# Pooled attention and grouped experts: K's sums turned by VectorE after a trip through DRAM, six weight buffers, halved subtractions, new orders

## The chip, the cores and the metric

The kernel runs on one core of one Trainium2 chip. The metric is the device time of one execution in microseconds (us); lower is better. Runs are compared with runs of the kernel before on the same chip.

## The reference, cut to what matters

Attention over pooled keys and values, then a layer of 16 experts in 4 groups, of which each token uses one:

```python
# q, k, v: (8 batches, 8 heads, 576, 64), float32
k_p = k.reshape(B, H, 72, 8, D).mean(axis=3)          # K and V pooled by 8
v_p = v.reshape(B, H, 72, 8, D).mean(axis=3)
scores = matmul(q, k_p.T) / 8
attn = exp(scores - max); attn /= attn.sum() + 1e-9
x = matmul(attn, v_p)  -> (4608 tokens, 512)
g = argmax(x @ w_group); e = argmax(x @ w_expert[g])   # the token's group and expert
out = softmax weight of g * softmax weight of e * (relu(x @ w1[g, e]) @ w2[g, e])
# w1[g, e]: 512 x 1024, w2[g, e]: 1024 x 512
```

## The kernel before

**Batches and pieces.** The work of a batch (576 tokens) is cut into pieces, methods of `Att` (attention and routing) and `Moe` (the experts). `main_expert` (L459) finds the expert that most tokens of the batch chose; `Moe` computes the whole batch with it. What other experts are owed is done at the end by `Left` in blocks of 32 rows. Three batches are in flight: in the strings that set the order, `a` and `m` are attention and experts of batch b, `n` and `w` those of b+1, `x` the attention of b+2, `t` the opening's odd jobs and `l` the leftover.

**Order.** Nothing is scheduled by the compiler. Four strings, `START`, `FIRST` (batch 0), `STEADY` (batches 1 to 6) and `LAST` (batch 7), name the pieces one by one, and each engine and each DMA queue takes its instructions in that order. An instruction that waits holds up everything behind it on its engine. Nearly all loads are issued by SP (SyncE), stores of the output by ScalarE's queue.

**K.** `load_k` fetches K; `kr` (L225, by `total`, L211) and `rr` (L230) sum 8 neighbours into `kp` and `rp`. For the scores, K must have the head dimension on the partitions: `kt` (L263) does that on TensorE, for batch 0 by matmuls against the identity, for the others by two transposes (L268) and two small matmuls (L264); `kta` (L277) brings the result to SBUF on ScalarE and scales it by 1/64 (L288, L292 for batches 1 to 7). `q` of batches 1 to 7 is loaded in pieces of 32 columns (`load_qb`, 4 DMAs of 72 KB a piece, L209) and turned by VectorE (`qb`, L309).

**The rest of the attention.** `sc` (L320) scores on TensorE; `mx`, `sb`, `su_` (L326, L333, L342 to L344) maximum, subtraction and sum on VectorE; `ex` (L337) the exponential on ScalarE; `nm` (L349) the division on POOL (GpSimd); `pt` (L355) a turn on VectorE. `vr` sums V and `rep` (L244, L247), `repa` (L253), `repd` (L261) spread it. `av` (L374) multiplies by V on TensorE; `ava` (L388) and `avd` (L392) split the result into two fp32r parts, `xr` (L399) adds them again on POOL into buffers of the pool `sw`, `rt` (L408) computes the routing's logits on TensorE, `route` (L425 to L449), `count` (L455, L457), `main_expert`, `elect` (L469 to L474) and `gates` (L510 to L521) are small VectorE steps. `elect` ends with a register that SP reads, from which the weight loads take the address.

**The experts.** A weight tile of 512 KB is loaded by `load` (L548, SP) into `sw` (4 buffers), `split` (L555, ScalarE) rounds it to fp32r into `wh`, `spd` (L560, VectorE or POOL) subtracts that into the rest `wl`. There are four tiles of w1 (`1:0` to `1:3`) and four of w2. `up` (L573) multiplies with three products a pair, in 8 rows `f` of two halves (256 and 320 tokens), into a PSUM pool `mm` of 3; `ua` (L578, ScalarE) and `upd` (L583, VectorE) evict it; rows 0 and 1 need tile `1:0`, 2 and 3 `1:1`, 4 and 5 `1:2`, 6 and 7 `1:3`. `down` (L612, L617) has 14 pieces of 8 matmuls, evicted by `da` (L625 to L631) through `y` (3 buffers) and stored. `half` (L586) is a `down` of one chunk for half the columns, used in the last batch. `warm` (L905) runs matmuls on ones.

```python
STEADY = """
m.up:0:0 m.split:1:3 m.ua:0:0 m.up:0:1 n.sc:1 n.qb:2 n.sc:2 n.qb:4 ...
... n.avd:0:0 x.kt x.rep n.avd:0:4 x.qb:0 x.kta n.xr:0 n.xr:2 ... n.rt x.sc:0 ... n.route ...
n.main_expert ... w.load:1:0 n.gex w.load:1:1 m.down:5 w.split:1:0 ... w.spd:1:0:v ... n.gates w.load:1:2 w.spd:1:1:p n.keep_x
"""
```

Of the kernel before, what the change touches and what calls it, by code (L numbers as in the profile page):

```python
# [49 lines left out]
m.load:2:1 m.up:7:1 m.load:2:0 m.split:2:3 n.vr:0 m.up:1:0 m.up:0:0 n.ex:2 n.sc:1 m.upd:6:0 a.rt n.qb:4 m.load:2:2 n.su_:2 n.rep n.sb:0 m.ua:7:1  # L50
m.upd:7:1 x.load_qb:3 n.mx:1 n.nm:2:p m.ua:0:0 n.pt:2 m.spd:2:3:p m.ua:1:0 m.upd:0:0 n.sb:1 m.up:6:1 n.qb:3 m.upd:1:0 n.repa:0 a.route n.ex:0
m.split:2:2 x.load_k:0 x.load_qb:0 m.up:3:1 x.load_k:1 m.ua:6:1 m.ua:3:1 n.ex:1 x.load_v:1 m.split:2:0 n.su_:0 a.count m.up:1:1 n.repa:1 m.up:2:1
m.upd:6:1 n.sc:3 n.repd:1 m.split:2:1 n.sc:4 m.ua:2:1 n.su_:1 m.up:0:1 a.keep_x m.ua:1:1 n.repd:0 n.nm:0:p m.upd:3:1 n.nm:1:p m.upd:2:1 m.spd:2:1:p
m.up:5:1 m.up:4:1 n.mx:4 n.pt:0 m.upd:1:1 n.mx:3 m.spd:2:0:p n.pt:1 m.down:0 n.sb:3 n.sb:4 m.ua:5:1 n.ex:3 m.ua:0:1 n.ex:4 m.ua:4:1 m.upd:5:1
m.upd:0:1 n.su_:4 m.spd:2:2:p n.nm:4:p m.upd:4:1 a.gex n.su_:3 n.nm:3:p m.down:12 x.kr:1:p n.pt:4 m.down:13 n.pt:3 n.av:0:4 x.load_qb:2 x.load_qb:1
n.ava:0:1 x.kr:0:r x.load_v:0 m.down:1 x.rr:r a.gates n.ava:0:4 n.ava:0:0 n.ava:0:3 n.ava:0:2 n.avd:0:4 n.avd:0:0 x.vr:1:p n.avd:0:3 m.da:4 n.avd:0:2
m.down:2 n.xr:0 m.down:9 n.xr:3 x.kt x.qb:0 n.ava:0:5 n.avd:0:1 n.avd:0:5 x.kta n.xr:2 m.down:6 x.vr:0:r x.sc:0 n.xr:1 n.rt x.rep x.mx:0 x.sb:0
# [5 lines left out]
m.up:0:0 m.split:1:3 m.ua:0:0 m.up:0:1 n.sc:1 n.qb:2 n.sc:2 n.qb:4 m.up:1:0 m.ua:0:1 x.load_k:1 m.upd:0:1 x.load_v:0 m.ua:1:0 m.up:2:0 x.load_k:0
m.up:1:1 m.ua:2:0 m.split:1:2 n.qb:3 n.mx:1 m.upd:1:0 m.spd:1:3 m.up:7:0 m.up:3:0 m.up:7:1 n.sc:3 m.upd:2:0 n.sb:1 m.ua:1:1 m.load:2:2 m.spd:1:2
m.upd:0:0 n.mx:2 n.sc:4 m.upd:1:1 n.ex:1 n.sb:2 m.ua:7:0 n.ex:2 n.su_:2 m.split:2:1 m.upd:7:0 n.su_:1 m.ua:3:0 m.up:4:0 m.upd:3:0 m.ua:7:1 m.up:4:1
n.mx:3 m.up:3:1 x.load_qb:0 n.nm:1:p m.load:2:3 m.ua:4:1 m.up:6:0 m.split:2:0 m.ua:3:1 m.upd:7:1 x.load_r:v n.nm:2:p m.spd:2:1:p n.pt:1 m.up:5:0
m.up:5:1 m.up:6:1 m.ua:6:0 n.mx:4 n.sb:3 m.up:2:1 m.upd:4:1 n.pt:2 m.ua:4:0 n.ex:3 m.upd:3:1 m.upd:6:0 n.sb:4 n.su_:3 m.spd:2:0 m.upd:4:0 n.ex:4
n.nm:3:p m.ua:5:0 n.su_:4 m.upd:5:0 m.split:2:2 n.pt:3 m.split:2:3 m.ua:2:1 x.load_r:k n.nm:4:p x.kr:1:p n.pt:4 m.ua:6:1 m.ua:5:1 n.av:0:4 n.ava:0:4
x.vr:0:p m.upd:2:1 m.spd:2:2 n.ava:0:3 m.upd:5:1 x.load_v:1 n.ava:0:0 x.vr:1:p x.rr:r x.load_qb:2 m.upd:6:1 x.load_qb:1 n.ava:0:5 m.down:6 m.down:0
n.avd:0:3 m.spd:2:3:v n.ava:0:2 m.down:7 n.ava:0:1 n.avd:0:1 n.avd:0:2 m.down:8 m.down:12 n.xr:3 n.avd:0:5 x.load_qb:3 m.da:2 m.down:1 n.xr:1 x.kr:0:r  # L70
# [7 lines left out]
l.step m.ua:5:0 l.step m.ua:1:1 m.upd:4:0 l.step m.ua:5:1 m.load:2:3 m.spd:1:3 m.up:6:0 m.upd:5:0 l.step m.split:2:0 m.up:4:1 m.spd:2:0:p l.step
m.ua:0:1 m.up:7:0 l.step l.step m.up:6:1 m.ua:6:0 l.tiles l.which m.split:2:3 m.upd:5:1 m.upd:1:1 m.split:2:2 m.split:2:1 m.upd:0:1 l.fetch_x m.up:7:1
l.fetch_b:1 m.ua:7:0 m.ua:6:1 m.ua:4:1 m.upd:6:0 m.spd:2:1:p m.spd:2:3:p m.ua:7:1 l.slots m.upd:7:0 m.upd:4:1 m.spd:2:2:v l.rows m.upd:6:1 m.down:3  # L80
l.whole:1 l.whole:3 m.down:4 m.down:5 m.upd:7:1 l.whole:0 m.da:1 l.whole:2 l.whole:4 l.turn:0 l.fetch_a:1 l.turn:1 l.turn:3 m.half:3:1 l.turn:2
# [874 lines left out]
```

## Time and profile before

| what | us |
|---|---|
| runs shown: median (lowest to highest of 3) | 559.41 (558.39 to 564.97) |
| the profiled execution | 561.18 |
| its span on the core | 559.1 |
| TensorE busy | 528.1 (94%) |
| VectorE, POOL, ScalarE busy | 364.8, 269.1, 211.7 |

The span goes from the first to the last instruction of the program; 2.1 us lie around it. Busy times are unions of the instructions' spans. A granted clock of 1.00 is full speed. A release behind an idle time ("<-") is inferred from semaphores. In the trace's times, 0 is the span's start.

### The profile page before, as it was taken

To read this page: it belongs to the slowest core of one execution; us is meant where nothing else is said; L and a number is where in the kernel's file an instruction comes from. 1 tells how busy PE (TensorE), PEld (TensorE's weight loads), DVE (VectorE), ACT (ScalarE), POOL (GpSimd) and SP (SyncE) were. 2 spreads that over 40 slices of the span, in tenths; PEclk is the share of its full clock that TensorE was granted. 3 is DMA by queue.
4 is the path that set the end of the run, shared out by engine and by line. 5 is a ranking of instruction groups with operands and counts; after the bars stand their busy time and mean duration, and the time that the engine had idled before them with its cause. 6 is when DMAs were issued, how large, how long until landed. Compare 5 with 4: busy or idle time off the path is not lost.

```text
span 559.1 us, 15184 instructions
## 1 busy us (share of the span) xinstructions
PE 528.1 (94%) x6218; PEld 471.0 (84%) x6218; DVE 364.8 (65%) x940; ACT 211.7 (38%) x402; POOL 269.1 (48%) x212
## 2 busy tenths in 40 slices
PE   3789999999999999999999999999997999979995
PEld 2689887799789998899789988899887987879874
DVE  4789898767656786587467786577667763237620
ACT  2254514454235441544235532545143441334202
POOL 3436395037904684247804593457704652344300
PEclk9679999999999999999999999999998999989999
DMA  9778551680528632781638441894354101724901
GB/s 233 157 192 211 134 111 50 237 284 9 123 64 287 174 71 69 236 240 32 118 109 310 107 93 49 275 335 113 70 184 148 39 2 39 255 94 158 340 12 54
DMA packets 115648, 81.32 MB, mean 145 GB/s; under 512 B 73562, under 2 KB 92250, under 8 KB 115192
## 3 DMA queue, kind: packets, MB, share of 16 engines
q1 hardware_dynamic: 110256, 70.92, 45.6%
...
## 4 chain that ended last, share of the span: by engine, by line
PE 86%; DVE 5%; DMA 4%; ACT 1%; issue 1%; POOL 1%; SPq 0%; ACTq 0%; POOLq 0%; DVEq 0%
PE mm L573 36%; PE mm L612 28%; PE mm L617 5%; PE sc L320 4%; PE sc L374 4%; DMA sw<-in_moe_w_dram 2%; PE tp L408 1%; DMA rem<-in_k_dram 1%; DMA ht<-in_moe_w_expert_dram 1%; PE mm L592 1%; PE sc L244 1%; PE mm L905 1%; PE tp L374 1%; ACT w L555 1%; DVE loh L518 0%
## 5 line engine op out<-in xcount | busy, mean ns | idle before, releaser
L573 PE MATMUL mm<-xt,w 128*128 128x320 f32 (+1 forms) x1536 | 214.6, 300 | 4.1 <-DVE ht L583 4.0
L573 PEld LDWEIGHTS mm<-xt,w 128*128 128x128 f32 x1536 | 208.3, 192 | 6.9 <-DVE ht L583 4.2
L612 PE MATMUL mm<-w,ht 128*128 128x512 f32 x744 | 176.7, 393 | 0.0
L612 PEld LDWEIGHTS mm<-w,ht 128*128 128x128 f32 x744 | 138.1, 188 | 30.9 <-issue 2.1
L560 POOL TENSOR_TENSOR w<-sw,w 128x1024 fp32r<-128x1024 f32 x47 | 113.0, 2413 | 95.8 <-ACT w L555 93.4
L349 POOL TENSOR_TENSOR p<-p,su 128x576 f32<-128x576 f32 (+1 forms) x40 | 45.8, 1150 | 135.4 <-DVE su L344 128.1
L578 ACT ACTIVATE ht<-mm 128x320 fp32r<-128x320 f32 (+1 forms) x128 | 49.5, 408 | 112.6 <-PE mm L573 112.4
L583 DVE SCALAR_TENSOR_TENSOR ht<-mm,ht 128x256 fp32r<-128x256 f32 (+1 forms) x192 | 59.7, 342 | 47.5 <-ACT ht L578 46.1
L555 ACT CAST w<-sw 128x1024 fp32r<-128x1024 f32 x64 | 65.9, 1043 | 27.4 <-DMA sw<-in_moe_w_dram 21.9
L625 ACT ACTIVATE y<-mm,gm 128x512 f32<-128x512 f32 x31 | 21.3, 687 | 69.8 <-PE mm L612 69.8
L399 POOL TENSOR_TENSOR sw<-xt 128x640 f32<-128x640 f32 (+1 forms) x28 | 39.9, 1455 | 7.3 <-DVE xt L392 7.3
L342 DVE TENSOR_REDUCE su<-p 128x8 f32<-128x576 f32 (+1 forms) x40 | 29.8, 744 | 15.2 <-ACT p L337 15.0
L309 DVE STREAM_TRANSPOSE qT<-q 128x512 f32<-128x512 f32 x35 | 24.4, 700 | 20.0 <-PE sc L320 15.1
L218 POOL TENSOR_TENSOR kv<-kv 128x512 f32<-128x512 f32 x21 | 31.9, 1517 | 10.3 <-DMA kv<-in_v_dram 7.9
L560 DVE TENSOR_TENSOR w<-sw,w 128x1024 fp32r<-128x1024 f32 x17 | 28.1, 1654 | 10.9 <-ACT w L555 10.9
L326 DVE TENSOR_REDUCE mx<-sc 128x8 f32<-128x576 f32 (+1 forms) x40 | 29.4, 735 | 6.1 <-PE sc L320 6.1
L355 DVE STREAM_TRANSPOSE pT<-p 128x576 f32<-128x576 f32 (+1 forms) x40 | 30.8, 769 | 3.1 <-POOL p L349 3.1
L617 PE MATMUL mm<-w,ht 128*128 128x512 f32 x128 | 32.4, 397 | 0.0
L337 ACT ACTIVATE p<-p 128x576 f32<-128x576 f32 (+1 forms) x40 | 27.3, 684 | 13.4 <-DVE p L333 9.8
L320 PE MATMUL sc<-kT,qT 64*64 64x72 f32 x1264 | 27.8, 235 | 4.5 <-DVE qT L309 2.9
L374 PE MATMUL sc<-pT,v 32*64 32x128 f32 (+11 forms) x1560 | 30.8, 290 | 1.2 <-DVE m L493 1.1
L320 PEld LDWEIGHTS sc<-kT,qT 64*64 64x64 f32 x1264 | 23.7, 139 | 9.6 <-DVE qT L309 3.1
...
## 6 DMA issues: line engine op xcount, KB each, us to landing
...
```

The lines of the kernel that those rows point to most:

```text
L218: add(out=a[..., 0:256], in0=a[..., 0:256], in1=a[..., 256:512], op=ALU.add)
L320: nc.tensor.matmul(ps[t:t + 64, y, SP * g:SP * g + SP], lhsT=s.qT[c][r, g, w:w + 64], rhs=k, start=True, stop=True)
L349: (nc.vector if eng == "v" else nc.gpsimd).tensor_tensor(out=pf, in0=pf, in1=bc(sf, SP), op=ALU.mult)
L374: nc.tensor.matmul(to[64 * x:64 * x + 64], lhsT=w, rhs=s.pT[e, k, 32 * c0:32 * c0 + n], start=(z == 0), stop=(z == 2))
L399: nc.gpsimd.tensor_tensor(out=x, in0=a, in1=b, op=ALU.add)
L555: nc.scalar.copy(out=wh, in_=raw)
L560: (nc.vector if eng == "v" else nc.gpsimd).tensor_tensor(out=wl, in0=raw, in1=wh.bitcast(F32), op=ALU.subtract)
L573: nc.tensor.matmul(ps[:, 0:n], lhsT=l[:, kc, fs], rhs=xt[:, r, kc, sl], start=(kc == 0 and i == 0), stop=(kc == 3 and i == 2))
L578: nc.scalar.activation(out=s.ht[f][:, o:o + n], in_=s.pu[f, hf][:, 0:n], func=AF.Relu)
L583: stt(out=ht[:, at:at + hi - lo], in0=ps[:, lo - o:hi - o], scalar=0.0, in1=ht[:, lo:hi].bitcast(F32), op0=ALU.max, op1=ALU.subtract)
L612: nc.tensor.matmul(ps, lhsT=s.ht[f][:, 640 * l + o:640 * l + o + 128], rhs=s.w[2, f // 2][r][:, f % 2, :], start=(i == 0), stop=(i == 23))
L617: nc.tensor.matmul(ps, lhsT=s.ht[f][:, 512:640], rhs=s.w[2, f // 2][r][:, f % 2, :], start=(i == 0), stop=(i == 15))
```

## The change

- From batch 1 on, `kt` and `kta` are no longer used. `kw` writes the sums of K to a DRAM buffer `kscr`, `kl` reads them back with 32 positions on the partitions, and `kb` turns them on VectorE in blocks of 32 x 32. `kw` and `kl` are issued by SP.
- 1/64 is no longer multiplied into K by `kta` but given to the exponential as its scale (`ex`), in batch 0 too.
- The pool `sw` has 6 buffers, not 4; `y` has 2, not 3.
- `spd` on POOL is two instructions, each half of the tile (for w1 the halves are the pairs of k chunks that `up` takes in order, for w2 the two rows `f`).
- `FIRST`, `STEADY` and `LAST` are new; `START` isn't changed. `t.warm:8` is no longer in `FIRST`.

```diff
 FIRST = """
-m.split:1:3 a.mx:2 m.up:2:0 n.load_qb:2 m.split:1:2 m.ua:2:0 a.sc:4 a.sb:2 t.warm:8 m.spd:1:2:p m.up:3:0 a.pt:3 m.up:4:0 m.up:5:0 a.ex:2 a.mx:4 a.sb:4
-a.ex:4 m.ua:5:0 n.load_qb:0 a.su_:2 a.nm:2:p a.su_:4 m.ua:3:0 a.nm:4:p m.upd:2:0 a.pt:2 m.split:1:0 a.pt:4 n.rr:r m.ua:4:0 x.load_r:k a.av:2:4
...
+n.load_qb:2 a.sc:4 m.split:1:2 m.split:1:3 a.mx:2 a.sb:2 a.pt:3 a.ex:2 a.mx:4 a.sb:4 m.spd:1:2:p m.split:1:0 m.spd:1:3:v a.su_:2 a.ex:4 n.rr:r
+m.up:3:0 a.su_:4 n.kw a.nm:2:p m.up:5:0 m.ua:3:0 m.ua:5:0 a.nm:4:p n.load_qb:0 m.upd:5:0 m.up:7:0 n.kl a.pt:2 x.load_k:1 m.ua:7:0 m.upd:7:0 m.up:2:0
+m.spd:1:0:p a.pt:4 m.ua:2:0 a.av:2:4 m.up:0:0 m.upd:2:0 a.ava:2:0 n.qb:2 a.ava:2:2 m.upd:3:0 a.ava:2:1 m.load:2:2 x.load_v:1 a.ava:2:3 m.up:1:0
+m.ua:1:0 n.load_v:0 a.avd:2:0 m.ua:0:0 x.load_r:v a.avd:2:2 x.kr:1:p m.load:2:0 a.avd:2:1 n.kb n.qb:1 a.avd:2:3 n.sc:2 m.upd:0:0 x.load_r:k n.sc:1
...
 STEADY = """
...
+m.up:1:0 x.load_qb:2 m.up:0:0 n.sc:1 m.split:1:2 m.ua:0:0 n.qb:2 n.sc:2 m.spd:1:2 m.up:3:0 m.up:4:0 m.ua:1:0 m.up:0:1 m.upd:0:0 m.upd:1:0 m.ua:3:0
...
+n.av:0:4 m.upd:6:1 x.rr:r n.ava:0:1 m.down:6 n.ava:0:4 m.upd:5:1 n.avd:0:1 m.down:12 m.upd:4:1 n.ava:0:5 x.vr:1:p x.load_k:1 m.spd:2:3:v m.down:7
+n.avd:0:4 n.ava:0:2 n.avd:0:5 n.ava:0:0 x.kr:1:p n.ava:0:3 m.down:3 n.xr:1 m.down:8 x.kr:0:r x.load_qb:1 m.da:2 m.down:4 x.load_qb:3 n.avd:0:3 x.rep
+x.repa:1 n.xr:3 n.avd:0:0 n.avd:0:2 n.xr:2 n.xr:0 n.rt n.route m.down:13 m.down:0 x.kw m.da:4 x.kl x.kb n.gex x.repd:1 n.main_expert w.load:1:0
+m.down:1 m.down:9 x.qb:1 x.qb:0 w.load:1:1 x.sc:0 x.mx:0 w.load:1:2 x.sb:0 x.repd:0 w.load:1:3 x.repa:0 x.ex:0 m.down:5 m.down:2 w.load:2:0
+w.split:1:0 m.da:1 m.down:10 m.down:11 n.gates x.su_:0 n.keep_x w.spd:1:0:v w.load:2:1 m.da:0 w.split:1:1 m.da:3 x.nm:0:p x.pt:0 w.spd:1:1:p
 LAST = """
-m.split:1:2 m.up:1:0 m.up:0:0 m.ua:1:0 m.up:3:0 m.up:2:0 m.ua:0:0 m.up:2:1 m.up:3:1 m.ua:3:0 l.xtiles m.split:1:3 l.step l.step m.spd:1:2:p m.up:4:0
...
+m.up:3:0 m.up:2:0 m.up:3:1 m.ua:3:0 m.split:1:3 m.ua:2:0 m.up:1:0 m.up:1:1 m.split:1:2 m.upd:2:0 l.xtiles m.ua:3:1 l.step m.ua:1:0 l.step m.spd:1:2:p
...
+m.down:8 l.fetch_b m.da:4 m.da:2 m.half:3:0
...
+    kscr = dram.tile([B, H * SP, D], F32, name="kscr")
-    sw = ctx.enter_context(tc.tile_pool(name="sw", bufs=4))
+    sw = ctx.enter_context(tc.tile_pool(name="sw", bufs=6))
...
+        def kw(s):
+            to = kscr[s.b].rearrange("(g r) d -> r g d", g=NG)
+            for u in range(2):
+                nc.sync.dma_start(out=to[0:128, u::2], in_=s.kp[:, 2 * u:2 * u + 2])
+            nc.sync.dma_start(out=to[128:144].rearrange("r g d -> g r d"), in_=s.rp[64:128])
+        def kl(s):
+            s.kn = wk.tile([128, 9, 32], F32, name="kn")
+            for y in range(2):
+                for e in range(2):
+                    r = 64 * y + 32 * e
+                    nc.sync.dma_start(out=s.kn[r:r + 32], in_=kscr[s.b, 288 * y:288 * y + 288].rearrange("(k t) d -> t k d", t=32)[:, :, 32 * e:32 * e + 32])
+        def kb(s):
+            s.kT = wk.tile([128, 4 * SP], F32, name="kT")
+            nc.vector.transpose(out=s.kT, in_=s.kn.rearrange("p k d -> p (k d)"))
...
-            nc.scalar.activation(out=p[0:n], in_=p[0:n], func=AF.Exp)
+            nc.scalar.activation(out=p[0:n], in_=p[0:n], func=AF.Exp, scale=1.0 / 64)
...
+            if eng == "v":
+                tt(out=wl, in0=raw, in1=wh.bitcast(F32), op=ALU.subtract)
+                return
+            z = raw.shape[1] // 2
+            for p in (slice(0, z), slice(z, 2 * z)):
+                nc.gpsimd.tensor_tensor(out=wl[:, p], in0=raw[:, p], in1=wh[:, p].bitcast(F32), op=ALU.subtract)
...
-            y = sm.tile([128, DM], F32, name="y", bufs=3)
+            y = sm.tile([128, DM], F32, name="y")
```

## Rows read from the trace of the kernel before

**Rows 1.** The page: busy times of the engines, and the granted clock in 40 slices.
```profile
PE 528.1 (94%) x6218; PEld 471.0 (84%) x6218; DVE 364.8 (65%) x940; ACT 211.7 (38%) x402; POOL 269.1 (48%) x212
...
PEclk9679999999999999999999999999998999989999
```

**Rows 2.** Windows: stretch, us, busy per engine (instructions), granted clock, DMA share, GB/s.
```profile
168.00:196.00 28.00, 28.00 (x308) 26.60 (x308) 19.73 (x52) 14.21 (x24) 15.34 (x8) 1.00 0.75 226
...
492.60:500.00 7.40, 7.40 (x46) 7.40 (x47) 1.04 (x4) 2.20 (x6) 3.69 (x2) 0.81 0.46 142
```

**Rows 3.** Waits of TensorE: released by: us in total, times, longest.
```profile
PE mm L298 <- DMA q<-in_q_dram: 7.7, 1, 7.7
PE mm L573 <- DVE ht L583: 4.0, 1, 4.0
...
PE sc L320 <- DVE qT L309: 2.9, 1, 2.9
...
PE tp L455 <- DVE oh L449: 0.8, 1, 0.8
```

**Rows 4.** The chain that ended last: start, us, what; batches 2, 6, 7.
```profile
177.33 9.47 PE mm L573 x72
...
426.37 10.95 PE mm L573 x72
...
492.56 6.46 PE mm L573 x36
```

**Rows 5.** Timeline of TensorE, batch 2: start, us, what.
```profile
215.77 0.38 PE L268 MATMUL tp<-ident,kp 128*128 128x128 f32 x2
216.08 0.33 PE L264 MATMUL tp<-ident,rp 64*64 64x64 f32 x4
216.34 0.71 PE L244 MATMUL sc<-vp,four 32*128 32x256 f32 x8
```

**Rows 6.** Timeline of VectorE, batch 2: start, us, what.
```profile
209.97 2.01 DVE L215 TENSOR_REDUCE kp<-kv 128x128 f32<-128x1024 f32 x1
...
218.63 0.32 DVE L425 STREAM_TRANSPOSE lg<-tp 128x128 f32<-128x128 f32 x1
...
223.44 0.22 DVE L457 TENSOR_REDUCE cnt<-tp 128x16 f32<-128x80 f32 x1
```

**Rows 7.** Timeline, batch 2, and the chain at 410 us: landings.
```profile
203.09 8.92 SPq L209 DMA_DIRECT2D q<-in_q_dram  x12
...
213.84 0.71 DVE L309 STREAM_TRANSPOSE qT<-q 128x512 f32<-128x512 f32 x1 [1.07 <-DMA q<-in_q_dram]
...
410.35 5.54 DMA sw<-in_moe_w_dram
```

**Rows 8.** Timeline of the opening: start, us, what.
```profile
30.71 14.61 SPq L209 DMA_DIRECT2D q<-in_q_dram  x16
...
38.50 2.05 PE L905 MATMUL mm<-ones 128*128 128x128 f32 x16
...
44.83 1.01 DVE L215 TENSOR_REDUCE rp<-rem 128x64 f32<-128x512 f32 x1
...
44.95 2.55 PE L374 MATMUL sc<-pT,v 32*64 32x96 f32 x192
...
51.12 1.23 PE L320 MATMUL sc<-kT,qT 64*64 64x72 f32 x64
```

**Rows 9.** Timeline around the end of batch 5: VectorE and POOL.
```profile
419.76 4.72 POOL L560 TENSOR_TENSOR w<-sw,w 128x1024 fp32r<-128x1024 f32 x2 [4.09 <-ACT w L555]
419.83 2.44 DVE L518 TENSOR_TENSOR loh<-oh,mp 128x80 fp32r<-128x80 f32 x1
...
422.45 2.04 DVE L521 TENSOR_TENSOR gm<-gm,gate 128x5 f32<-128x5 f32 x1
```

**Rows 10.** Timeline at the end of batch 6: loads, and the last tile's split.
```profile
475.21 12.14 SPq L548 DMA_DIRECT2D sw<-in_moe_w_dram  x6
...
490.45 1.04 ACT L555 CAST w<-sw 128x1024 fp32r<-128x1024 f32 x1 [5.38 <-DMA sw<-in_moe_w_dram]
```

More of the change, by code (lines that the diff above doesn't have):

```diff
@@ L50 @@
[L50 to L57, printed above, removed]
@@ new lines @@
+x.load_qb:0 a.route m.ua:3:1 n.ex:0 m.split:2:0 m.upd:3:1 m.up:5:1 n.su_:1 n.repa:1 m.upd:4:0 n.su_:0 m.ua:4:1 a.gex m.upd:4:1 m.split:2:1 m.load:2:3
+m.up:0:1 n.repd:0 n.repa:0 m.spd:2:0:p m.ua:0:1 n.sc:3 n.nm:0:p m.spd:2:2:p n.sc:4 m.ua:5:1 n.repd:1 m.spd:2:1:p x.kr:0:r a.count n.mx:3 n.nm:1:p
+m.upd:5:1 m.up:6:1 m.ua:6:1 n.pt:0 m.upd:0:1 n.sb:3 m.upd:6:1 x.load_qb:3 n.ex:3 a.keep_x m.up:1:1 m.ua:1:1 m.down:0 m.split:2:3 n.su_:3 n.pt:1
+m.upd:1:1 n.mx:4 n.sb:4 n.nm:3:p x.qb:0 m.up:2:1 m.ua:2:1 n.ex:4 x.qb:1 m.down:9 m.spd:2:3:p m.down:1 x.load_v:0 n.su_:4 n.pt:3 n.nm:4:p x.rr:r
@@ new lines @@
+x.vr:1:p m.down:2 n.pt:4 m.upd:2:1 n.av:0:4 m.down:10 n.ava:0:0 n.ava:0:2 n.ava:0:5 n.ava:0:1 m.down:11 a.gates n.avd:0:2 n.avd:0:0 x.kw m.down:3
+m.down:12 x.kl n.avd:0:5 n.ava:0:4 n.avd:0:1 n.ava:0:3 n.avd:0:3 n.avd:0:4 x.kb n.xr:2 n.xr:1 n.xr:0 m.da:0 n.xr:3 x.vr:0:r n.rt x.sc:0 n.route m.da:3
+m.down:13 n.main_expert x.mx:0 w.load:1:0 x.sb:0 w.load:1:1 x.ex:0 m.down:4 m.da:4 m.down:6 n.gex x.rep m.down:7 x.su_:0 w.load:1:2 w.load:1:3
+x.repa:0 m.down:5 w.load:2:1 w.load:2:0 n.gates x.repd:1 x.repd:0 x.nm:0:p w.split:1:0 m.da:1 w.spd:1:0:v n.keep_x m.down:8 x.pt:0 w.split:1:1 m.da:2
@@ L61 @@
+w.spd:1:1:v x.repa:1
 """
 STEADY = """
[L63 to L70, printed above, removed]
@@ L78 @@
[L78 to L81, printed above, removed]
@@ L82 @@
-l.turn:4 l.gather m.down:0 l.next_ l.back m.half:3:0 l.up m.down:12 l.hback m.down:1 l.fetch_a l.fetch_x m.down:2 l.down l.slots m.down:13 m.down:6
-m.da:0 l.fetch_b m.down:7 m.down:8 m.da:4 m.da:2
+m.up:3:0 m.up:2:0 m.up:3:1 m.ua:3:0 m.split:1:3 m.ua:2:0 m.up:1:0 m.up:1:1 m.split:1:2 m.upd:2:0 l.xtiles m.ua:3:1 l.step m.ua:1:0 l.step m.spd:1:2:p
+m.ua:1:1 m.up:5:0 m.spd:1:3 m.up:7:0 m.upd:3:0 m.up:4:0 m.upd:3:1 m.ua:5:0 m.ua:4:0 m.load:2:2 m.load:2:3 m.upd:1:0 m.upd:1:1 m.up:0:0 m.up:2:1
+m.up:5:1 m.up:6:0 m.ua:7:0 l.step l.step l.step m.ua:2:1 m.ua:0:0 m.upd:5:0 m.up:4:1 m.split:2:1 m.ua:5:1 l.step l.step l.step m.split:2:2 m.ua:6:0
@@ new lines @@
+m.upd:4:0 m.up:7:1 m.ua:4:1 l.step m.spd:2:1:p m.split:2:0 l.step l.tiles m.ua:7:1 m.up:0:1 m.spd:2:0:p m.upd:7:0 m.up:6:1 l.which m.upd:0:0 m.upd:2:1
+l.fetch_x l.fetch_b:1 m.split:2:3 m.spd:2:3:p m.upd:5:1 m.down:0 m.upd:6:0 l.slots m.ua:6:1 m.upd:4:1 m.upd:7:1 m.spd:2:2:v m.upd:6:1 l.rows l.whole:1
+m.down:1 m.down:3 l.whole:3 l.whole:0 l.whole:2 l.whole:4 l.turn:0 l.fetch_a:1 l.turn:1 l.turn:3 m.ua:0:1 m.down:4 l.turn:2 l.turn:4 l.gather m.down:5
+m.upd:0:1 m.da:1 l.next_ l.back m.half:3:1 l.up m.down:6 l.hback l.fetch_a m.down:12 l.fetch_x m.down:2 l.down l.slots m.down:13 m.down:7 m.da:0
@@ L273, in kt @@
                     nc.tensor.matmul(ps[64 * y:64 * y + 64, 128 * g:128 * g + 128], lhsT=s.kp[:, 2 * (g % 2) + g // 2], rhs=ident, start=True, stop=True)
-            ps = s.tk2 = ps_m.tile([128, 512], F32, name="mm")
-            tail(ps)
+            s.tk2 = ps_m.tile([128, 512], F32, name="mm")
+            for a in range(2):
+                nc.tensor.matmul(s.tk2[64 * a:64 * a + 64, 256:320], lhsT=s.rp[64:128], rhs=ident[64:128, 64:128], start=True, stop=True)
         def kta(s):
-            ps = s.tk
@@ L622, in da @@
             ps = s.pd[c]
[L623 removed]
+            y = sm.tile([128, DM], F32, name="y")
             if n == 128:
```

44 lines of the change are left out of this document (13 added, 31 removed).

## The prediction

> **What bounds the kernel now.** I read the page first: TensorE is busy for 528.1 of 559.1 us, no other engine for more than 65%, and its clock is at full speed except in the opening and for single slices near the end [rows 1]. A steady stretch such as 168 to 196 us has no idle TensorE time at all [rows 2]. So inside a batch only instructions taken off TensorE shorten the kernel, and what else can be won or lost is the 31 us in which TensorE waits. TensorE's list of waits shows where: 7.7 us on the first q in the opening, which the change leaves alone; 4.0 us on `upd` (L583); 2.9 us on a turn of q (L309); 0.8 us on the routing [rows 3]. Each of the two long waits is followed by matmuls at a lower clock: 72 `up` matmuls took 10.95 us behind the 2.9 us wait and 9.47 in a steady batch; 36 took 6.46 behind the 4.0 us wait where half of 9.47 would be 4.74 [rows 4]. In 492.6 to 500 the granted clock is 0.81, a mean of the two levels 1.2 and 2.4 GHz [rows 2]. So the 2.9 us wait cost 2.9 + 1.5 = 4.4 us and the 4.0 us wait 4.0 + 1.7 = 5.7.
>
> The sum goes against the profiled execution, 561.18 us with a span of 559.1. The median of the runs is 559.41, 1.8 below it; I take the difference off the median.
>
> **The turn of K off TensorE.** For batches 1 to 7 `kt` puts two transposes (L268) and two small matmuls of two passes each (L264) on TensorE. In the steady batch they begin at 215.77 and the next group, L244, begins at 216.34: 0.57 us [rows 5]. Seven of them are 4.0 us. ScalarE loses `kta`'s three scalings; it isn't the bound, so nothing is counted. The new fold of 1/64 into the exponential's scale adds no instruction. In their place stand `kw` (3 DMAs), `kl` (4 DMAs, which must wait on SP until `kw` has landed) and `kb` (one VectorE turn of 288 columns). The turn: 128 columns took 0.31 us [rows 6], 512 took 0.71 [rows 7], so 0.5. The round trip has no row. DMAs of the same kind (72 KB in pieces of 128 bytes) took SP 8.92 us for twelve, 0.74 each, and the turn waiting on the last began 1.83 us after that issue ended, at 213.84 [rows 7]. So: 3 x 0.74 + 1.83 + 4 x 0.74 + 1.83 = 8.8, and 9.3 with the turn. The far bound for a landing is 5.54 us from issue, for the weight tile at 410.35 [rows 7]; the near bound is nothing. I take 1.83, since size and pattern are nearest.
>
> In a steady batch that is covered. `kb` stands on VectorE after the routing and ahead of `main_expert`, with everything that elects the expert behind it. In the kernel before, K's sum (L215) ended at 211.98 and `main_expert`'s first VectorE step (L457) ran at 223.44 [rows 6]: 11.5 us for a trip of 9.3, so 2.1 spare. Behind the waiting `kl` on SP there are only loads that need the elected expert anyway. But with `kt` gone TensorE reaches `rt` 0.57 us earlier, and the chain of `avd` and `xr` that `rt` needs gets no shorter: between none and all of the 0.57 comes back as a wait. The third `y` buffer is also taken away, so an eviction of 0.69 or so may wait for an earlier store. I take 0.4 of 0.57 back (bounds 0 and 1.2). Five steady batches, 1 to 5: 5 x (-0.57 + 0.4) = -0.9.
>
> **The opening.** Here the trip isn't covered. SP issues 16 q DMAs from 30.71 on, in 14.61 us, 0.91 each [rows 8]; after twelve (`load_qb` 3, 1, 2) it is 41.7. `kw` waits for `rr`, which the new order puts on VectorE ahead of `su_:4`, not behind both `pt`: by VectorE's own row order I estimate its end at 43.0 (it began at 44.83 before [rows 8]). Then 3 x 0.64, the fourth `load_qb` (4 x 0.91), `kl` (4 x 0.74), a landing of 1.83 and the turn: 43.0 + 1.9 + 3.65 + 2.95 + 1.83 + 0.5 = 53.9. TensorE's list has only two `up` halves between `av` and `sc:2`. `av` itself gets later: a subtraction of 1.2 us moved to VectorE and `rr`'s 1.0 now stand in front of `su_:4`, half a us is won because `sc:4` is first, so about 46.5 where it was 44.95; it ends 2.55 later, two halves of 1.5 bring 52.0, and TensorE waits 1.9 for `kb`. `sc:2` then starts at 53.9 where it started at 51.12 [rows 8], with the same work behind it: +2.8 us. With a trip that costs nothing it would be 52.0, +0.9; with two landings of 5.54, about +10. The dropped warm-up (16 matmuls, 2.05 us [rows 8]) is no gain in this sum, since TensorE waits for `av` in its place; without it the pauses may let the clock fall, for which I take one of the drops priced above, +1.5 (bounds 0 and 3). The Trainium skill (TensorE: Matmul & The Clock Gate, What's actually happening) says that the array gets half its clock when it has not been busy; the 0.81 row agrees that a pause is followed by it, and by that rule the 1.5 would come for certain.
>
> Rest of the first batch: -0.57 for the second `kt`; `count` now follows `rt` behind one score group and one `down` only, so its wait of 0.8 [rows 3] grows, +0.5 (0 to 2); `n.load_v:0` waits in the new order for a buffer that `n.vr:1` frees late, so `rep` may wait, +0.5 (0 to 2); `rt` behind four `down`s where six stood, +0.3. Together +0.7. Opening and first batch: 2.8 + 1.5 + 0.7 = +5.0.
>
> **The 2.9 us wait.** It stood at the end of batch 5. The first weight tile came 5.54 us after its issue, and then `gates` stood on VectorE between its subtraction and `n.qb:2`: `loh` took 2.44 us and `gm` 2.04, for steps that do 80 and 5 columns, each ending with one of POOL's two subtractions of 2.36 (419.76, 4.72 for two) [rows 9]. The new order puts `gates` ahead of the subtraction, so nothing but `pt:0` is left behind it: gone even when the tile is late, -4.4. What is late next is the second tile's subtraction on POOL, in halves ready 1.2 us sooner. The halves add between nothing and 1.2 us a tile on POOL, 48% busy [rows 1]; no cost.
>
> A rule bears on the halves. The rows say that VectorE was held until POOL's instruction ended [rows 9]. The Trainium skill (SBUF — State Buffer, Who interferes with whom) says that a VectorE operation with two SBUF inputs and a GpSimd operation that reads SBUF exclude each other for the whole instruction, the first to start winning. By that a row of several such VectorE steps is held once per half, so the halves alone would win little and the reordering has to do it.
>
> **The 4.0 us wait.** Six weight tiles were issued from 475.21 over 12.14 us, because four buffers were shared with `xr`; the last, `1:2`, came at 490.45, and its `split` was first on ScalarE in the last batch, ahead of every `ua` [rows 10]. TensorE ran out of PSUM tiles. Six buffers let the six loads go out at once, and `LAST` puts `ua:3:0` ahead of `split:1:3` and `1:2`. Late next: `LAST` begins with `up:3:0`, whose subtraction on POOL follows a `split` behind two evictions: I estimate 0.7 us of waiting (0 to 3), too short to count a drop of the clock. -5.7 + 0.7 = -5.0.
>
> **The end.** The last eviction is of 256 columns, not 512: -0.2.
>
> **Sum**: +5.0 - 0.9 - 4.4 - 5.0 - 0.2 = -5.5 us; 561.18 becomes 555.7, the median 559.41 becomes 553.9. I say **554**, own range 550 to 558, chance 0.50.
>
> **Rivals.** (1) *The trip is hidden in the opening too* (0.22). For it: no row shows such a small landing at its dearest. Opening +0.9, no clock drop, rest -0.57, steady between -0.9 and -2.9: 559.4 + 0.3 - 0.9 - 9.6 = 549.2 down to 547.2; time 548. (2) *The waits at the ends come back* (0.21): the late tile rather than the order of ScalarE was the cause, or the loads, now six in a row, land later. Half of the 9.4 stays, the opening loses its 5.0: 558.6; all of it stays: 563. Against it: the rows name the steps that stood between. Time 560. (3) *Slower* (0.07): the landing in DRAM and the reading back take long in every batch. `kb` then holds `main_expert` on VectorE, the weight loads come late and TensorE runs dry at each batch's end. It decides from a landing of 1.83 + 2.1/2 = 2.9 us each. At 5.54 each `main_expert` is 5.3 late; five times, with the opening's further 7.4: 554 + 26 + 7 = 587. Against it: q's landing row. The Trainium skill (DMA: Bandwidth & Descriptors, Anatomy of one DMA) says that the end of a DMA can come surprisingly late when it writes to HBM; no row here shows a wait for such a write.
>
> **Range and chances.** 546.5 to 563 takes in the likeliest case and the first two rivals. A measurement of this kernel tells about 2%, 11.2 us, from no change: below 548.2 is faster, half of rival 1 and a tail of the likeliest, 0.17; above 570.6 slower, rival 3 and a little, 0.08; between, 0.75.
>
> **What would show it.** Right: no L268 and no L264 after batch 0; a TensorE wait of 1 to 3 us at the first L320 group near 54 us, released by the VectorE turn of `kn`; batches of 60.8 to 61.2 us; no wait over 1 us near batch 6 and the last batch, and the clock 1.00 there. Wrong: the turn of `kn` waiting on a DMA in steady batches; `value_load` on SP later after `rt` than before; a wait at the start of `LAST` released by POOL.

## The result, and the profile after

The changed kernel takes 562.62 us (median of 20 runs, 561.06 to 567.46), the kernel before 559.4 beside it: ratio 1.0057, 95% interval 1.0037 to 1.0078. So 3.2 us were lost where 5.5 were to be won. The time lies in the range that was given, but near its upper end, and not for the reason that put the end there: that it lies inside is luck.

The profiled execution spans 560.9 us, 1.8 more than the one before. I cut both at the first `up` of each batch (from TensorE's timeline; the opening, with batch 0's experts, ends where batch 1's begin). First the windows between these cuts for the kernel before: stretch, length, busy time and instructions of TensorE, its weight loads, VectorE, ScalarE, POOL, then granted clock, DMA share, GB/s.

```profile
0.00:110.61 110.61, 95.47 (x1510) 83.49 (x1511) 88.71 (x217) 41.62 (x83) 52.58 (x60) 0.92 0.65 163
...
172.81:234.00 61.19, 61.18 (x709) 54.95 (x708) 42.71 (x107) 25.57 (x49) 33.81 (x24) 1.00 0.52 148
...
418.71:483.95 65.24, 61.31 (x660) 54.65 (x658) 39.20 (x107) 23.50 (x43) 25.28 (x14) 0.97 0.27 89
483.95:559.10 75.15, 64.56 (x511) 57.76 (x509) 28.38 (x100) 19.66 (x38) 24.45 (x19) 0.96 0.39 136
```

The same windows of the kernel after:

```profile
0.00:113.98 113.98, 94.37 (x1483) 82.51 (x1483) 87.52 (x213) 39.85 (x76) 53.02 (x66) 0.91 0.66 160
...
176.16:239.75 63.59, 62.10 (x703) 54.69 (x702) 42.83 (x108) 24.95 (x46) 34.73 (x31) 1.00 0.54 150
239.75:304.16 64.41, 62.13 (x704) 54.56 (x702) 41.93 (x108) 24.80 (x45) 33.81 (x31) 1.00 0.53 144
...
365.92:430.03 64.11, 62.28 (x703) 54.73 (x702) 41.63 (x108) 24.91 (x45) 33.84 (x30) 1.00 0.62 183
430.03:490.03 60.00, 59.66 (x659) 53.28 (x658) 33.39 (x95) 23.16 (x42) 26.26 (x21) 1.00 0.27 89
490.03:560.90 70.87, 63.79 (x511) 56.59 (x509) 28.43 (x100) 19.16 (x37) 24.55 (x25) 0.97 0.42 148
```

| stretch | before | after | difference | predicted |
|---|---|---|---|---|
| opening and first batch | 110.6 | 114.0 | +3.4 | +5.0 |
| five steady batches (1 to 5) | 308.1 | 316.05 | +7.95 | -0.9 |
| batch 6 | 65.2 | 60.0 | -5.2 | -4.4 |
| last batch and end | 75.15 | 70.87 | -4.3 | -5.2 |

Three terms have the right sign and about the right size in these two executions. The fourth is wrong: steady batches take 61.8 to 64.4 us in place of 61.2 to 62.3. The clock is not the reason; it is 1.00 in all of them. The windows show the form of the loss: batch 2 had no idle TensorE time before (61.18 of 61.19) and now has 1.5 us, and its busy time grew by 0.9 though K's six matmuls are gone.

The page row of the engines, which answers to [rows 1], then TensorE's waits (released by: us in total, times, longest), which answer to [rows 3]:

```profile
PE 527.6 (94%) x6160; PEld 465.4 (83%) x6160; DVE 361.7 (64%) x947; ACT 207.5 (37%) x381; POOL 271.5 (48%) x259
```

```profile
PE mm L302 <- DMA q<-in_q_dram: 7.5, 1, 7.5
PE mm L582 <- DVE ht L592: 3.8, 6, 1.8
...
PE mm L582 <- POOL w L569: 3.1, 12, 0.3
```

The 4.0 and 2.9 us waits are gone. New are twelve waits for `w` on POOL, one or two in each batch. No single one is over 0.3 us, so a list sorted by the longest would hide them. Sorting all matmuls by kind and taking each from its start to the next one's start (my working on the timeline) gives, for the five batches together: `up` +5.6 us, `down` +2.9, `av` +2.1, scores +0.3, and the rest, where `kt` stood, -2.9; sum +7.95.

What is late is seen on ScalarE. Its waits, one row:

```profile
ACT y L634 <- DMA out_dram<-y: 16.3, 6, 4.0
```

and the join of batches 1 and 2 on ScalarE, with its DMA issues (start, us, what, idle time before and its releaser):

```profile
173.68 0.34 ACTq L635 DMA_DIRECT2D out_dram<-y  x1
...
175.22 1.05 ACT L559 CAST w<-sw 128x1024 fp32r<-128x1024 f32 x1 [0.41 <-ACT y L634]
178.90 0.69 ACT L634 ACTIVATE y<-mm,gm 128x512 f32<-128x512 f32 x1 [2.62 <-DMA out_dram<-y]
179.61 0.34 ACTq L635 DMA_DIRECT2D out_dram<-y  x1
179.99 1.05 ACT L559 CAST w<-sw 128x1024 fp32r<-128x1024 f32 x1 [0.41 <-ACT y L634]
```

POOL and TensorE in the same stretch:

```profile
176.35 2.54 POOL L569 TENSOR_TENSOR w<-sw,w 128x512 fp32r<-128x512 f32 x2 [1.79 <-PE mm L621]
181.12 5.04 POOL L569 TENSOR_TENSOR w<-sw,w 128x512 fp32r<-128x512 f32 x4 [2.23 <-ACT w L559]
```

```profile
180.28 1.94 PE L582 MATMUL mm<-xt,w 128*128 128x256 f32 x13
182.46 0.98 PE L582 MATMUL mm<-xt,w 128*128 128x256 f32 x6 [0.24 <-POOL w L569]
183.71 3.46 PE L582 MATMUL mm<-xt,w 128*128 128x256 f32 x24 [0.27 <-POOL w L569]
```

Read from right to left: TensorE waits for POOL's subtraction of `1:2`; POOL had been idle for 2.23 us, since the `split` of `1:2` (L559) started at 179.99; ScalarE had come to it late, because the eviction of `da:3` (L634) stood in front and waited 2.62 us for a store two evictions earlier to leave its `y` buffer. With three buffers that store had one more eviction's time. A store is issued at 173.68 here and its buffer comes free at about 178.9, 5.2 us later, too late for the next eviction but one in the new order; in the old orders, experiment 3, it is in time but for once.

### The profile page after: what moved, and what is told of

Same layout as the page of the kernel before. It is cut to its first block, busy times and chain, and to the rows that moved or that the text cites. A ratio compares the mean times of both kernels' runs of the same rounds, so it can differ in the third digit from the quotient of the medians.

```text
span 560.9 us, 15145 instructions
## 1 busy us (share of the span) xinstructions
PE 527.6 (94%) x6160; PEld 465.4 (83%) x6160; DVE 361.7 (64%) x947; ACT 207.5 (37%) x381; POOL 271.5 (48%) x259
## 4 chain that ended last, share of the span: by engine, by line
PE 71%; DVE 9%; DMA 6%; POOL 5%; issue 5%; ACT 1%; SPq 1%; POOLq 0%; ACTq 0%; DVEq 0%
PE mm L582 27%; PE mm L621 25%; POOL w L569 5%; PE mm L626 5%; PE sc L378 4%; PE sc L324 2%; DMA sw<-in_moe_w_dram 2%; PE tp L412 2%; DMA rem<-in_k_dram 1%; DMA out_dram<-y 1%; DMA ht<-in_moe_w_expert_dram 1%; PE mm L601 1%; DVE pT L359 1%; DVE su L346 1%; DVE ht L592 1%
## 5 line engine op out<-in xcount | busy, mean ns | idle before, releaser
L582 PE MATMUL mm<-xt,w 128*128 128x320 f32 (+1 forms) x1536 | 217.2, 299 | 7.0 <-DVE ht L592 3.8
L621 PE MATMUL mm<-w,ht 128*128 128x512 f32 x744 | 178.8, 394 | 0.2 <-DVE ht L592 0.2
L569 POOL TENSOR_TENSOR w<-sw,w 128x512 fp32r<-128x512 f32 x94 | 120.6, 1307 | 69.6 <-ACT w L559 50.4
L592 DVE SCALAR_TENSOR_TENSOR ht<-mm,ht 128x256 fp32r<-128x256 f32 (+1 forms) x192 | 59.2, 345 | 63.5 <-ACT ht L587 62.7
L559 ACT CAST w<-sw 128x1024 fp32r<-128x1024 f32 x64 | 66.7, 1044 | 11.1 <-DMA sw<-in_moe_w_dram 6.1
L634 ACT ACTIVATE y<-mm,gm 128x512 f32<-128x512 f32 x31 | 21.4, 689 | 71.2 <-PE mm L621 50.7
L403 POOL TENSOR_TENSOR sw<-xt 128x512 f32<-128x512 f32 (+1 forms) x28 | 39.1, 1428 | 11.4 <-DVE xt L396 11.4
L219 POOL TENSOR_TENSOR kv<-kv 128x512 f32<-128x512 f32 x21 | 27.1, 1288 | 25.6 <-DMA kv<-in_k_dram 17.7
L378 PE MATMUL sc<-pT,v 32*64 32x128 f32 (+12 forms) x1560 | 32.0, 294 | 4.5 <-issue 3.1
L429 DVE STREAM_TRANSPOSE lg<-tp 128x128 f32<-128x128 f32 x8 | 2.5, 314 | 48.5 <-PE tp L412 48.5
L378 PEld LDWEIGHTS sc<-pT,v 32*64 32x64 f32 (+3 forms) x1560 | 28.2, 142 | 5.8 <-issue 4.6
L626 PE MATMUL mm<-w,ht 128*128 128x512 f32 x128 | 32.8, 398 | 0.0
L337 DVE TENSOR_TENSOR p<-sc,mx 128x576 f32<-128x576 f32 (+1 forms) x40 | 29.6, 740 | 0.5
```

The costliest lines, as they stand in the source:

```text
L378: nc.tensor.matmul(to[64 * x:64 * x + 64], lhsT=w, rhs=s.pT[e, k, 32 * c0:32 * c0 + n], start=(z == 0), stop=(z == 2))
L403: nc.gpsimd.tensor_tensor(out=x, in0=a, in1=b, op=ALU.add)
L559: nc.scalar.copy(out=wh, in_=raw)
L569: nc.gpsimd.tensor_tensor(out=wl[:, p], in0=raw[:, p], in1=wh[:, p].bitcast(F32), op=ALU.subtract)
L582: nc.tensor.matmul(ps[:, 0:n], lhsT=l[:, kc, fs], rhs=xt[:, r, kc, sl], start=(kc == 0 and i == 0), stop=(kc == 3 and i == 2))
L592: stt(out=ht[:, at:at + hi - lo], in0=ps[:, lo - o:hi - o], scalar=0.0, in1=ht[:, lo:hi].bitcast(F32), op0=ALU.max, op1=ALU.subtract)
```

## Experiments

Twelve kernels, in three groups, each group beside runs of the kernel before. Ratios are to these, with 95% intervals. "Theory Y" and so on are named in the expectations.

**1. A third `y` buffer (e1_y3).** The six weight buffers stay; for all but the last two batches every third `y` is a slice of a tile that stands idle there.

```diff
-            y = sm.tile([128, DM], F32, name="y")
+            y = s.ytile()
...
+        def ytile(s):
+            turns[0] = (turns[0] + 1) % 3
+            if turns[0] == 2 and s.b < B - 2:
+                return pp.tile([128, NG, S], F32, name="pl").rearrange("p g i -> p (g i)")[:, 0:DM]
+            return sm.tile([128, DM], F32, name="y")
```

> The kernel after with a third y buffer again for batches 0 to 5; it lies in a tile that only the last batch uses (pl). Theory Y (the eviction da:3 waits on ScalarE for the store of two evictions before, and the split of weight tile 1:2 and the ua's stand behind it): the 16.3 us that ScalarE waits for stores go to under 5, the 60 up matmuls after sc:2 take 7.8 us in every batch where they took 8.35 to 9.48, and the kernel is 4 to 6 us faster than the one after: 557 to 558.5. Theory H (POOL's halved subtractions are late by themselves): no change, 562.6, and TensorE still waits for L569 in every batch. Theory L (six loads in a row come late): no change, 562.6.

Measured 556.99 us, ratio 0.9923 (0.989 to 0.9957): from 0.57% slower than before to 0.77% faster by this one buffer, 7.5 us by the two ratios, more than expected. The same two rows of waits:

```profile
ACT y L640 <- DMA out_dram<-y: 3.9, 1, 3.9
PE mm L582 <- POOL w L569: 0.5, 2, 0.3
```

The stores' waits fell from 16.3 to 3.9 us, TensorE's on POOL from 3.1 to 0.5; what is left of both stands in the last batch, which has two buffers here too. That is theory Y; H and L, which expected no change, are out as they were stated. The five steady batches take 310.7 us in place of 316.05; `up` alone won 4.4 of that. This is more than the listed idle time that went: around the two waits of 0.24 and 0.27 us in batch 2 of the kernel after, one matmul and the next start 0.62 and 0.55 us apart, where 0.14 is usual in such a row (my working on the timeline).

**2. Two buffers, but the `split` ahead of the waiting eviction (e2_split_first).** For batches 1 to 5:

```diff
- w.split:1:1 m.da:3 x.nm:0:p x.pt:0 w.spd:1:1:p
+ w.split:1:1 w.split:1:2 m.da:3 x.nm:0:p x.pt:0 w.spd:1:1:p
...
-m.split:1:2
```

> The kernel after, two y buffers, but at the ends of batches 1 to 5 the split of tile 1:2 is put ahead of da:3 on ScalarE. Theory Y: da:3 still waits as long, but POOL gets tile 1:2 earlier; the waits of TensorE for L569 go, those for the ua's behind da:3 stay: 1.5 to 4 us faster than the kernel after, 558.5 to 561. Theory H: no change or 1 us. Theory L: no change, since the tile itself would be late.

Measured 557.71, ratio 0.9927 (0.99 to 0.9955), as good as e1_y3; I had expected less.

```profile
ACT y L634 <- DMA out_dram<-y: 14.3, 7, 4.1
...
PE mm L582 <- POOL w L569: 1.2, 4, 0.4
```

The evictions still wait 14.3 us, and it costs next to nothing. So the wait is not the price; what is queued behind it is. In the profile both splits now run as one group of two, from 176.27 on, and only then does `da:3` wait:

```profile
176.27 2.00 ACT L559 CAST w<-sw 128x1024 fp32r<-128x1024 f32 x2 [0.41 <-ACT y L634]
179.79 0.69 ACT L634 ACTIVATE y<-mm,gm 128x512 f32<-128x512 f32 x1 [1.52 <-DMA out_dram<-y]
```

**3. Two buffers in the kernel before (e3_before_y2).**

```diff
-            y = sm.tile([128, DM], F32, name="y", bufs=3)
+            y = sm.tile([128, DM], F32, name="y")
```

> The kernel before with two y buffers and nothing else. Theory Y in its wide form (a third buffer is needed in any order): 2 to 6 us slower than before, 561 to 565. In its narrow form (it is the new order, with three evictions within some 6 us and six loads in flight beside the stores, that needs it): within 1 us of before, 559 to 560.

Measured 558.52, ratio 0.9967 (0.993 to 1.0004). In the old orders the third buffer is worth nothing that can be told from no change: ScalarE waits for a store once, 1.7 us. That is not due to the four weight buffers of this kernel: e8_old_orders_new_last below, with two `y` and six weight buffers, also waits for a store once, 3.5 us. Buffer and order cost only together. This run also shows something of the kernel before: its batch 6 takes 60.7 us, not 65.2, and its TensorE list has no wait of 2.9 us at the join of batches 5 and 6:

```profile
417.02 3.36 PE L573 MATMUL mm<-xt,w 128*128 128x256 f32 x24
420.31 1.23 PE L320 MATMUL sc<-kT,qT 64*64 64x72 f32 x64
421.47 2.77 PE L573 MATMUL mm<-xt,w 128*128 128x256 f32 x21
```

**4. POOL's subtraction whole (e4_whole; e9_y3_whole with the third buffer).**

```diff
-            z = raw.shape[1] // 2
-            for p in (slice(0, z), slice(z, 2 * z)):
-                nc.gpsimd.tensor_tensor(out=wl[:, p], in0=raw[:, p], in1=wh[:, p].bitcast(F32), op=ALU.subtract)
+            nc.gpsimd.tensor_tensor(out=wl, in0=raw, in1=wh.bitcast(F32), op=ALU.subtract)
```

> The kernel after with POOL's subtraction in one instruction again. Theory H: 2 to 4 us faster than the kernel after. Theory Y: where tile 1:2 is late behind da:3 each whole subtraction hands it over 1.1 us later than the first half does, in five batches: 2 to 6 us slower, 564.5 to 568.5.

> The changed kernel with the third y buffer (e1_y3) and Pool's subtraction whole again. Theory H (a half frees a matmul earlier only where a weight is late): with no eviction late, TensorE waits for Pool's w at the last batch's start alone, 2.0 us as in e8_old_orders_new_last, plus at most 0.5 per steady batch: time 2 to 4 us over e1_y3. Rival A (the new steady orders rest on halves): TensorE's waits on Pool's w stay at the 9.3 us that e4_whole showed, time 5 us or more over e1_y3.

e4_whole: 567.55, ratio 1.0113 (1.0073 to 1.0154), against 1.0057 with halves; the two intervals just touch. TensorE's wait for POOL:

```profile
PE mm L580 <- POOL w L567: 9.3, 8, 1.4
```

e9_y3_whole: 561.56, ratio 1.0019 (0.9986 to 1.0053), against 0.9923 with halves, some 5 us; the wait:

```profile
PE mm L580 <- POOL w L567: 6.4, 8, 1.8
```

The wait lies between the two theories, the time at rival A's: from batch 2 to batch 6 `up` takes 26.89 us in each where it took 26.32 in e1_y3, longer by just the 0.57 us that TensorE waits for POOL in each, so the new steady orders do rest on the halves, in every batch and not at the last one's start alone. I had priced the halves at nothing.

**5. K of batch 1 on TensorE (e5_kt_b1).** To the third buffer's kernel `kt1` (two transposes, two small products) and `kta1` (ScalarE's copies) were added, after the pattern of the old `kt` and `kta`.

```diff
- n.kw
...
- n.kl
...
- n.kb
+ n.kt1 n.kta1
```

> The changed kernel with the third y buffer (e1_y3, 557.0) in which K of batch 1 alone is turned on TensorE, as in the kernel before, and does not go through DRAM. Theory T (the trip is late in the opening): TensorE's wait of 0.59 us for kT in front of sc:2 goes and the scores start that much earlier, less the two transposes and two small products (0.5 to 0.6 us of TensorE): opening 0.5 us longer to 1.5 shorter than the 114.7 of e1_y3, time 555.5 to 557. Rival O (the order of the opening costs the 4 us, not the trip): opening within 0.5 us of 114.7, and TensorE's other waits in the opening (upd 1.8 us, av 46.8) stay. Both leave the steady batches at 61.4 to 62.8 us.

Measured 557.71, ratio 0.9953 (0.9926 to 0.998); opening 114.2 us. TensorE's timeline, first of the kernel after, then of this one:

```profile
44.24 2.60 PE L582 MATMUL mm<-xt,w 128*128 128x256 f32 x12 [1.83 <-DVE ht L592]
46.77 3.11 PE L378 MATMUL sc<-pT,v 32*64 32x96 f32 x192
49.81 3.12 PE L582 MATMUL mm<-xt,w 128*128 128x256 f32 x24
53.52 0.73 PE L324 MATMUL sc<-kT,qT 64*64 64x72 f32 x32 [0.59 <-DVE kT L296]
```

```profile
44.20 2.56 PE L598 MATMUL mm<-xt,w 128*128 128x256 f32 x12 [1.83 <-DVE ht L608]
46.70 3.16 PE L394 MATMUL sc<-pT,v 32*64 32x96 f32 x192
...
53.94 1.37 PE L340 MATMUL sc<-kT,qT 64*64 64x72 f32 x64 [0.53 <-ACT kT L294]
```

Without the trip the scores start no earlier. The opening's loss is put down to its order: `upd` (L592) waits on VectorE behind `rr` and `su_:4`, TensorE stands for 1.83 us, and `av` comes at 46.8 in place of 44.95 [rows 8].

**6. K of batches 3 to 7 on TensorE (e6_kt_steady).**

```diff
-n.avd:0:3 x.rep
+n.avd:0:3 x.kt1 x.rep x.kta1
...
- x.kw m.da:4 x.kl x.kb n.gex
+ m.da:4 n.gex
```

> The changed kernel with the third y buffer (e1_y3) in which the steady batches turn the next K on TensorE (x.kt1, x.kta1) in place of the trip through DRAM; batch 2's K and batch 1's still go through DRAM. Theory G (the turn's 0.57 us of TensorE is real gain in each steady batch once nothing else is late): batches 2 to 5 longer by 0.5 to 0.6 us each, time +2 to +3 against e1_y3 (557.0), 559 to 560. Rival N (TensorE has slack at the batch's end that the turn filled, or the trip's traffic costs as much): within 0.7 us of e1_y3.

Measured 558.98, ratio 0.9981 (0.9956 to 1.0006). Beside e5_kt_b1 of the same group, which has the trip in these batches, it is 1.3 us slower, and by ratio 3.2 slower than e1_y3. That speaks for theory G, that the turn off TensorE is a true gain once nothing else is late; the intervals overlap or touch, so its size is not settled.

**7. Four weight buffers (e7_sw4).** This is e1_y3 with one more edit:

```diff
-    sw = ctx.enter_context(tc.tile_pool(name="sw", bufs=6))
+    sw = ctx.enter_context(tc.tile_pool(name="sw", bufs=4))
```

> The changed kernel with the third y buffer (e1_y3) and four weight buffers, as before, in place of six. Theory S (the shorter last batch needs the loads that two more buffers start earlier): the last batch 3 to 4 us longer than the 70.8 of e1_y3, with TensorE waiting for a weight, time 560 to 561. Rival P (the new order of the last batch does it, whatever the buffers): within 0.7 us of e1_y3's 557.0.

Measured 556.55, ratio 0.9953 (0.9927 to 0.9979), the same as e5_kt_b1 beside it; the last batch 70.6 us. Rival P: the orders do it, and the two buffers that took the room of the third `y` buy nothing. They even delay the stores (last section).

**8. The kernel before with the new `LAST`: e8_old_orders_new_last** (six weight buffers, two `y`, subtraction whole) **and e12_new_last_halves** (four, three, halves). In both the `LAST` list is the one of the change, and no other list is touched; e8 also has the edit of experiment 3 and `bufs=6` for `sw`, e12 the change's `spd`.

```diff
 LAST = """
-m.split:1:2 m.up:1:0 m.up:0:0 m.ua:1:0
+m.up:3:0 m.up:2:0 m.up:3:1 m.ua:3:0 m.split:1:3
...
```

> The kernel before with only the last batch's order and the six weight buffers of the change, and two y buffers to make room (which alone measured 558.5 beside 560.7); K on TensorE and Pool's subtraction whole, all other orders as before. Theory L (the last batch's 4 us stand by themselves): the last batch 71 to 72 us in place of 75, time 4 to 5 us under the kernel before, ratio 0.991 to 0.993. Rival H (the last batch needs the subtraction in halves or what batch 6 leaves behind): 0 to 2 us under, and TensorE waits for POOL's w at the last batch's start.

> The kernel before with two parts of the change alone: the last batch's order and Pool's subtraction in halves; four weight buffers, three y buffers, K on TensorE. Theory L (all that the change wins is there, all that it loses is not): the last batch 70.5 to 71.5 us, the opening and the steady batches as before, time 4 to 5 us under the kernel before, 554.5 to 556, ratio 0.991 to 0.993. Rival Q (the halves cost Pool two starts for each weight and delay the steady batches): 0 to 2 us under before.

e8: 557.73, ratio 0.9959 (0.9926 to 0.9992), last batch 72.7 us: 2.0 us under the kernel before by the medians, 2.3 by the ratio, where theory L expected 4 to 5, and with the wait on POOL that rival H named. e12: 555.81, ratio 0.992 (0.9882 to 0.9959), last batch 72.2 us, longer than expected, its time as expected. TensorE at the last batch's start, first of e8, then of e12:

```profile
486.89 3.33 PE L573 MATMUL mm<-xt,w 128*128 128x256 f32 x14 [2.04 <-POOL w L560]
```

```profile
485.90 0.98 PE L578 MATMUL mm<-xt,w 128*128 128x256 f32 x6 [0.96 <-POOL w L565]
487.14 4.09 PE L578 MATMUL mm<-xt,w 128*128 128x256 f32 x19 [0.26 <-POOL w L565]
```

The 4.0 us wait goes with the order of `LAST` alone; a wait on POOL takes part of its place, and the halves shorten that one from 2.04 to 1.22 us in two pieces. The remaining 1.6 us to e7_sw4's 70.6 I put down to the new end of batch 6; no run has that alone.

**9. The old opening: e10_old_first and e11_old_first_sw6.** e7_sw4 with the whole `FIRST` of before, `kt` and `kta` in it as `kt1` and `kta1`; e11 the same with six weight buffers.

```diff
 FIRST = """
-n.load_qb:2 a.sc:4 m.split:1:2 m.split:1:3 a.mx:2
+m.split:1:3 a.mx:2 m.up:2:0 n.load_qb:2 m.split:1:2 m.ua:2:0 a.sc:4 a.sb:2 t.warm:8
...
```

> e7_sw4 (third y buffer, four weight buffers, new steady and last orders) with the first batch's order of before, K of batches 1 and 2 turned on TensorE in it. Theory F (the change's opening costs 4 us by its order, 114.7 to 115.1 us to the first product of batch 1 where before has 109.8 to 110.6): opening 110 to 111.5 us, time 552 to 553.5. Rival V (the opening varies by some us from one execution to the next, as e8_old_orders_new_last with the old order at 113.5 suggests): time within 1.5 us of e7_sw4, 555 to 557.

> e10_old_first with six weight buffers. Theory B (the two more buffers let loads run beside the opening's own and slow it): 2 to 3 us over e10_old_first, with the opening at 113 to 114 us as in e8_old_orders_new_last. Rival N (the buffers do nothing to the opening): within 1 us of e10_old_first.

e10_old_first: 551.89, ratio 0.9874 (0.9823 to 0.9926), the fastest of all, 1.3% under the kernel before and 1.8% under the changed one. Its page and two of its windows, opening and batch 2:

```profile
PE 527.1 (96%) x6188; PEld 466.5 (85%) x6188; DVE 360.3 (66%) x945; ACT 208.6 (38%) x387; POOL 270.6 (49%) x259
```

```profile
0.00:110.42 110.42, 96.48 (x1510) 84.28 (x1511) 89.00 (x217) 41.52 (x83) 53.35 (x66) 0.95 0.67 163
...
172.30:233.66 61.36, 61.28 (x703) 54.43 (x702) 42.00 (x108) 24.91 (x45) 33.84 (x31) 1.00 0.57 152
```

e11_old_first_sw6: 554.05, ratio 0.9909 (0.9877 to 0.994), opening 112.7. The 2.2 us between the two fit theory B, but the intervals overlap and the opening moves by itself: over the six profiled executions with the old `FIRST` it is 109.8 to 114.5 us, mean 111.9 (e12_new_last_halves, with four buffers, has the 114.5), over the eight with the new one 113.6 to 115.4, mean 114.4. Theory F holds with 2.5 us by these means and 4.4 by the ratios of e7_sw4 and e10_old_first; whether six buffers slow the opening stays open.

## Why the prediction was wrong

**The step that failed** is the steady batch: "The third `y` buffer is also taken away, so an eviction of 0.69 or so may wait for an earlier store. I take 0.4 of 0.57 back (bounds 0 and 1.2)." The edit and the wait were seen; the size was not. I took the eviction's own length for the size of its wait, and asked only what the waiting eviction delays, not what stands behind it on its engine. The wait is set by the store's 5.2 us and not by the eviction's 0.69 (and the store is that late in part because the change's six weight buffers let more loads go ahead of it, last section), and behind it on ScalarE stand the `split` and, on POOL, the subtraction of the weight that TensorE needs next. Measured: +1.6 us per batch in place of -0.17. e1_y3 takes 5.4 us of the 7.95 away by the buffer, e2_split_first shows that the queue behind the wait is what costs, and e3_before_y2 that the old order could bear it. The rest is 2.6 us: 1.1 of it is `av`, mostly its stalls (last section), the other 1.5 are the sum of K's -2.9, `down`'s +3.2 and `up`'s +1.2, the next two points.

**The turn of K: right.** 0.57 us of TensorE went in each batch, and the trip is hidden. In batch 2 on SP (`kw` L284 and L285, `kl` L292) and on VectorE (`kb`, no wait in front, as in every batch but the opening's):

```profile
215.99 0.90 SPq L284 DMA_DIRECT2D kscr<-kp  x2
216.93 0.61 SPq L285 DMA_DIRECT2D kscr<-rp  x1
218.86 1.82 SPq L292 DMA_DIRECT2D kn<-kscr  x4
```

```profile
227.99 0.46 DVE L296 STREAM_TRANSPOSE kT<-kn 128x288 f32<-128x288 f32 x1
```

The writes land 1.3 us after their last issue ends, and the issue of the last read ends 7.3 us ahead of the turn. Rival 3, late landings in every batch, is thereby false.

**What took it back: wrong in kind.** I expected a wait for the routing's inputs. Instead `down` grew by 3.2 us over five batches of e1_y3 and `up` by 1.2, together 4.4 against K's 2.9. The new lists break the `down`s into four pieces where there were three. From start to start, eight matmuls inside a piece take 1.81 us and the first eight of a piece 1.92 to 1.99, in the old lists 1.93 to 1.98; the last eight take about 1.91 or 2.05 in three of the four new pieces, and 1.81 or 1.82 in the old ones. In the kernel after, one more start makes 0.8 us of five batches and the slower ends 2.1, which is all of `down`'s 2.9 there. Why the ends are slower was not traced, nor was `up`'s 1.2.

**The opening: right in size, wrong in cause.** +3.4 where +5.0 stood (2.5 by the means of experiment 9), and the scores at 53.52 where I had 53.9. But the sum gave 1.9 of its 2.8 us to the trip; TensorE waited 0.59 for it, and e5_kt_b1 shows that the turn on TensorE costs as much in that place. The new order costs, as e10_old_first shows. `av` at 46.5 (46.77 came) was the part that was right, and more than this should have been laid on it. The 1.5 us for the clock is not shown by itself: from 42 to 56 us the granted clock is 0.88 where it was 1.00, but over the whole opening it is 0.99 in e1_y3, which takes 114.7 us, and 0.91 here with 114.0.

**The 2.9 us wait: right in mechanism, wrong in what it was worth.** It is gone, and batch 6 has the clock 1.00. But four executions of old orders had 65.2, 60.7, 61.7 and 61.3 us for batch 6: the wait stands in one of these four alone, with its weight tile that came 5.54 us after its issue [rows 7]. Against the mean of the other three the change wins 1.2 us there, not 4.4. That fits the medians, which differ by 3.2 us where the profiles differ by 1.8.

**The 4.0 us wait: right,** -4.3 for the last batch and the end against -5.2, but by the order of `LAST` and, it seems, the end of batch 6; the six buffers that I named have no part in it (e7_sw4). The sign of being wrong that I gave, a wait on POOL at the start of `LAST`, came too, with 0.5 us in two pieces. A store's wait of the same kind stands in this batch, of 4.0 us, but TensorE waits only 0.45 us behind it. The chain that ended last:

```profile
486.57 6.43 DMA out_dram<-y
```

**The halves: wrong.** Priced at nothing, they win about 3 us (e4_whole) to 5 us (e9_y3_whole) in the new orders. The rule that I weighed there, from the Trainium skill (SBUF — State Buffer, Who interferes with whom), would have them win little; it speaks of VectorE held by POOL, while the gain here is TensorE's, which can start on the first half.

Rival 2 gave a time near the measured one, by waits at the ends that would come back. They didn't; its time came out by another way, by luck.
